# A decode step of two attention and MLP layers: kept V comes back from PSUM through ScalarE, and q is spread beside the preceding unit

## The chip, the cores and the metric

The kernel runs on one core of one Trainium2 chip. The metric is the device time of one execution in microseconds, lower is better. Where one number stands for a kernel, it is the median of its runs.

## The reference

Two layers A and B are each applied twice, with the same weights and the same caches both times. A is one decode step of attention over a cache of 4096 positions, B a small MLP block.

```python
B, D = 8, 448;  Hq, Hkv, Sk, Dh = 16, 8, 4096, 256         # bf16
def A(x, k_cache, v_cache, wq, wo):
    q = (x @ wq) as [B, 16, 1, 256]
    scores = q . k_cache[b, head // 2] * Dh ** -0.5         # two q heads share a K/V head
    p = softmax(scores)
    return (p . v_cache[b, head // 2]) as [B, 1, 4096] @ wo
def Bk(x, w1, w2, w3, w4):                                   # S == 1: the shifted branch through w1, w2 is zero
    x1 = x
    return x1 + gelu(layernorm(x1) @ w3) @ w4
x = x + A(layernorm(x));  x = x + Bk(layernorm(x))
x = x + A(layernorm(x));  x = x + Bk(layernorm(x))
```

K and V of one batch row are 16.8 MB each. Both passes need all of them, and SBUF holds about one pair of K/V heads' worth at a time beside the weights, so nearly everything is read from HBM twice.

## The kernel before

**Units, chunks, items.** A *unit* is `(ps, b, gp)`: pass 0 or 1, batch row b, and one of four pairs of K/V heads (`GP = 4`). K and V of a unit are cut into four chunks of 1 MB each, `[128, 4096]` bf16. An *item* is `(n, kv, c)`: unit number n, K (0) or V (1) or a weight block (2), and chunk c. The list `items` is the order of all work, 527 items, written out ahead of time by `block`, `weights` and `first_kept`; the main loop walks it once. Each engine executes its instructions in the order in which this loop issues them.

**Places.** 17 places in SBUF (`NC = 17`, tile `places`) hold one chunk each. `emit_loads` runs at the end of every item. It sends the next loads of the list `loads` to free places, all from SyncE's queue (L839 for a pair of K chunks in two neighbouring places, 2 MB; L870 for one chunk; L873 for halves of a chunk; L867 and L868 for the chunk called `part`). A load waits in SyncE's queue until the last reader of its place is done, and everything behind it in that queue waits too. Where two K chunks of a unit shall lie side by side (`paired`), `place_for` holds back until two neighbouring places are free.

**What is kept from pass 0 to pass 1.** Of the units with gp 2 and 3 (`keep`), pass 1 of a row follows soon after its pass 0, so their data stay: 14 chunks in places (`kept`, asked for with `stays`), chunk 1 of V of gp 2 (`inner`) whole in the PSUM banks `store[0..3]`, and 6 of the 16 position groups of chunk 0 of V of gp 3 (`part`) in `store[4]` and half of the bank `sc`, while the other 10 groups lie in the SBUF tile `rest`. `away` and `part_away` (L937, L958) copy them into PSUM with VectorE transposes of 32-bit words in pass 0, after the chunk's own PV. `back` and `part_back` (L944, L962) copy them back with the same transposes in pass 1. They are called together, after the scores of chunks 0 and 1 of unit gp 2:

```python
            if (ps, gp, c) == (1, keep[0], 1):
                where[(b, part[0]), part[1:]] = part_place
                part_back(slots[part_place])
                where[(b, inner[0]), inner[1:]] = kept_place
                back(slots[kept_place])
```

The two places for that (`kept_place`, `part_place`) are those of K chunk 0 of gp 2 and K chunk 2 of gp 3, which are not given to new loads in the meantime.

**One unit.** For a K chunk that was loaded, VectorE transposes it in place in 32x32 blocks (L902, three instructions per chunk). TensorE computes scores into the bank `sc` (L917): 32 matmuls of 256 columns where two chunks lie in neighbouring places, and twice 32 matmuls of 128 columns otherwise. After every second chunk ScalarE does exp out of `sc` (L926). Then TensorE transposes P into the bank `misc` (L969), ScalarE copies it out (L976) and prepares P of one V chunk at a time in `ptw` (L1108), one V chunk ahead, and TensorE does the PV product with 16 matmuls (L986). Before a unit's scores, `give_q` lays out its q in one of four tiles `qbd`: four small matmuls into `misc` (L370), then four VectorE casts out of it (L376). One such layout serves two units.

**A batch row's round.** The units with gp 0 and 1 of several rows are read ahead. Then come gp 2 and 3 of the row in pass 0, and a run of V chunks loaded in halves (`narrow`), during which TensorE also works through the row's generator `chain`: normalising the heads, wo, the MLP, layer norms and the next q (L174, L529 and others; its `step` is called between the items). Then gp 3 and gp 2 of the same row follow in pass 1 out of what was kept, and their V chunks are interleaved with the next unit's K. For rows 3, 5, 7 and the last, a weight block wq is loaded again and q of earlier rows is computed in between (`weights("q", ...)`, L350, L885 to L892).

Of the kernel before, what the change touches and what calls it, by code (L numbers as in the profile page):

```python
# [10 lines left out]
U32 = mybir.dt.uint32  # L11
# [6 lines left out]
def kernel(  # L18
# [621 lines left out]
    AFTER = 10  # L640

    def block(k, v=None):

        fresh = [(number[v], 1, c) for c in range(4)] if v else []
        if k is None:
            due.extend(fresh)
            items.extend(due)
            due.clear()
            return
        number[k] = len(tasks)  # L650
        tasks.append(k)
# [97 lines left out]
    def late(it):  # L749

        n, kv, c = it
        return kv == 0 and paired(n, c) and not (tasks[n][0] == 1 and stays(it))

    used_at = {it: k for k, it in enumerate(items)}
    for it in items:
# [5 lines left out]
    for b in range(Bn):  # L761
        again[(b, keep[0]), 0, 0] = again[(b, inner[0]), *inner[1:]]
        again[(b, keep[1]), 0, 2] = again[(b, part[0]), *part[1:]]
    free_at = [-1] * NC
# [168 lines left out]

    def away(slot):

        for n in range(4):
            nc.vector.transpose(  # L937
                store[n][:].bitcast(U32), slot[:].bitcast(U32)[:, 512 * n : 512 * n + 512]
            )

    def back(slot):

        for n in range(4):
            nc.vector.transpose(  # L944
                slot[:].bitcast(U32)[:, 512 * n : 512 * n + 512], store[n][:].bitcast(U32)
            )

    def part_words(slot):

        w = slot[:].bitcast(U32)  # L950
        return [
            (sc[:, 256 : 256 + 128 * (PR - 4)], w[:, 512 : 128 * PR]),
            (store[4][:], w[:, 0:512]),
        ]

    def part_away(slot):
        for kept_words, words in part_words(slot):
            nc.vector.transpose(kept_words.bitcast(U32), words)  # L958

    def part_back(slot):  # L960
        for kept_words, words in part_words(slot):
            nc.vector.transpose(words, kept_words.bitcast(U32))  # L962

# [106 lines left out]

    def give_q(who):

# [16 lines left out]
        q_of[k] = who  # L1089
        run(spread_q(who[1], who[2], qbds[k]))  # L1090

# [3 lines left out]
    v_items = [it for it in items if it[1] == 1]  # L1095
    v_next = dict(zip(v_items, v_items[1:]))
    plain = {it for it in v_items if (tasks[it[0]][:2] == (1, Bn - 1)) and tasks[it[0]][2] in free}

# [14 lines left out]
    for idx, it in enumerate(items):  # L1113
# [20 lines left out]
        if kv == 2:  # L1134
# [9 lines left out]
            elif c == 1:  # L1144
# [15 lines left out]
                )  # L1160
                project_rows(q_of_block, 0, *rows, ps_q)
        elif kv == 0:
            if (ps, b) not in state:
# [15 lines left out]
            if not kept_now:  # L1179
                transpose_k(slot)  # L1180
            if not alone:
                step(idx)
# [26 lines left out]
        else:  # L1209
            st = state[ps, b]  # L1210
            if it in narrow and it[2] == 0 and not alone and any(e["kind"] == "chain" for e in gens):
                alone.append(n)
# [26 lines left out]
            else:  # L1239
# [5 lines left out]
                alone_now = (ps, b) in split and gp in free  # L1245
                if c == 0:
                    o_of[n] = st["o", g8]
                o_now = o_of[n]
                if c == 0 and (alone_now or pairs_done.get((ps, b), 0) % 2 == 1):
                    done = pairs_done[ps, b] + 1  # L1250
# [20 lines left out]
                if ps == 0 and inside(it):  # L1271
                    away(slot)
                if ps == 0 and halfway(it):
                    part_away(slot)
            if c == 3:
                pairs_done[ps, b] = pairs_done.get((ps, b), 0) + 1
                free_slots.append(slot_of.pop(n))
# [176 lines left out]
```

## Time and profile before

| | |
|---|---|
| median of 3 runs | 1065.47 us (1064.1 to 1067.35) |
| profiled execution | 1061.72 us, its span 1059.6 us |
| busy: TensorE, VectorE, ScalarE | 627.0, 616.4, 161.7 us of the span |
| mean granted TensorE clock | 0.678 |
| read from HBM | 424.22 MB, 400 GB/s over the span |

The profile is one execution on the chip. Its times are in us, those of single instructions in ns. In a group's row stand the line, the engine, the operation, what it writes and reads, the count, the busy time and the mean of one, and then the engine's idle time just before such instructions with what ended it. PE is TensorE, PEld its weight loads, DVE VectorE, ACT ScalarE, POOL GpSimd, SP SyncE, and SPq what SyncE's queue does. The chain is the work that ended last, followed back from the end.

### The profile page before, as it was taken

The numbers are of one execution on the slowest core, as the hardware profiler recorded it, in microseconds if no ns is written. First come the engines' busy times: TensorE is split into PE (matmuls) and PEld (weight loads), VectorE is DVE, ScalarE is ACT, GpSimd is POOL, SyncE is SP. The second block draws the span as 40 slices with busy tenths as digits, with TensorE's granted clock in tenths as the row PEclk, the third lists the DMA queues.
The fourth block names the chain that finished last, engine by engine and source line by source line (L and its number), as shares of the span: only waits on it lengthen the run. The fifth ranks groups of instructions, "written<-read, shape, count | busy, mean of one in ns | idle before, by whom it ended". The sixth has DMA issues, their size and how long they took to land.

```text
span 1059.6 us, 29163 instructions
## 1 busy us (share of the span) xinstructions
PE 627.0 (59%) x12932; PEld 395.0 (37%) x12932; DVE 616.4 (58%) x1319; ACT 161.7 (15%) x613; POOL 16.4 (2%) x27
## 2 busy tenths in 40 slices
PE   3144457655575547664586566656764666657675
PEld 2022225432343324442343234423442444434455
DVE  5146862578527882467628952785288437792362
ACT  1011110211111111111112111111111111111110
POOL 0000000000000000000000000000000000000000
PEclk9999996665675656657656566656665686556665
DMA  9999999999999999999999999999999999999994
GB/s 300 387 424 424 424 415 388 422 421 423 401 406 426 424 420 404 409 403 424 414 389 426 425 410 410 378 425 412 401 424 423 393 389 420 423 418 348 393 416 203
DMA packets 71757, 426.11 MB, mean 402 GB/s; under 512 B 7496, under 2 KB 13520, under 8 KB 43856
## 3 DMA queue, kind: packets, MB, share of 16 engines
q1 hardware_dynamic: 71440, 424.01, 98.8%
q8 instruction: 101, 1.65, 0.6%
q10 hardware_dynamic: 192, 0.25, 0.1%
q14 instruction: 24, 0.20, 0.0%
HBM read 424.22 MB, written 0.01 MB: 400 GB/s over the span
## 4 chain that ended last, share of the span: by engine, by line
DMA 47%; DVE 24%; PE 21%; ACT 3%; issue 2%; SPq 2%; POOL 1%; DVEq 0%; ACTq 0%
DMA places<-in_A_v_cache_dram 25%; DMA places<-in_A_k_cache_dram 20%; DVE places L902 18%; PE sc L917 9%; PE o L986 7%; ACT p_n L926 2%; PE misc L174 2%; DMA places<-in_A_wq_dram 2%; PE misc L529 1%; DVE store L937 1%; DVE places L944 1%; DVE qbd L376 1%; SPq L193 1%; SPq L870 1%; ACT o_sb L523 1%
## 5 line engine op out<-in xcount | busy, mean ns | idle before, releaser
L902 DVE STREAM_TRANSPOSE places<-places 128x512 uint32<-128x512 uint32 (+1 forms) x576 | 455.5, 854 | 83.0 <-DMA places<-in_A_k_cache_dram 81.0
L917 PE MATMUL sc<-places,qbd 128*8 128x256 bf16 (+1 forms) x5024 | 246.9, 347 | 244.9 <-DVE places L902 236.1
L986 PE MATMUL o<-places,ptw 128*8 128x256 bf16 x3808 | 232.3, 369 | 101.4 <-DMA places<-in_A_v_cache_dram 70.9
L917 PEld LDWEIGHTS <-qbd 128*8 128x8 bf16 x5024 | 130.4, 104 | 327.8 <-DVE places L902 140.1
L986 PEld LDWEIGHTS <-ptw 128*8 128x8 bf16 x3968 | 103.7, 102 | 171.4 <-issue 95.8
L926 ACT ACTIVATE p_n<-sc 128x256 bf16<-128x256 f32 x128 | 95.4, 745 | 395.1 <-PE sc L917 392.4
L1108 ACT COPY ptw<-psv 128x32 bf16<-128x32 bf16 x248 | 52.6, 226 | 173.7 <-PE o L986 161.4
L976 ACT CAST psv<-misc 128x128 bf16<-128x128 f32 x64 | 17.0, 266 | 253.3 <-PE misc L969 253.3
L493 DVE RECIPROCAL rz<-misc 128x8 f32<-128x8 f32 (+1 forms) x35 | 6.7, 191 | 77.4 <-PE misc L490 77.4
L376 DVE CAST qbd<-misc 32x32 bf16<-32x32 f32 x128 | 23.2, 182 | 27.6 <-PE misc L370 26.3
L529 PE MATMUL misc<-R_t,o_sb 128*128 128x8 f32 (+1 forms) x132 | 26.7, 311 | 20.7 <-DVE R_t L515 13.9
L529 PEld LDWEIGHTS misc<-R_t,o_sb 128*128 128x128 f32 x132 | 23.8, 252 | 30.9 <-issue 17.2
L926 ACT ACTIVATION_READ_ACCUMULATOR p_n<-sc 128x1 f32 x128 | 33.8, 264 | 0.0
L174 PEld LDWEIGHTS <-w_sb 128*128 128x128 bf16 x896 | 27.3, 103 | 14.2 <-issue 13.8
L525 DVE MEMSET o<- 128x256 f32 x33 | 9.0, 272 | 35.0 <-PE o L986 31.2
L490 PE MATMUL misc<-zm,one 128*128 128x8 f32 (+1 forms) x70 | 17.1, 317 | 18.9 <-DVE zm L482 17.1
L275 POOL TENSOR_TENSOR t<-t,nhalf 128x2 f32<-128x2 f32 (+2 forms) x18 | 12.0, 670 | 957.7 <-DVE t L296 957.7
L490 PEld LDWEIGHTS misc<-zm,one 128*128 128x128 f32 x70 | 14.1, 251 | 29.1 <-issue 24.9
L969 PEld LDWEIGHTS <-p_n 128*128 128x128 bf16 x256 | 11.9, 105 | 31.6 <-issue 20.0
L969 PE MATMUL misc<-identb,p_n 128*128 128x32 bf16 x256 | 18.0, 190 | 9.3 <-ACT p_n L926 6.8
L937 DVE STREAM_TRANSPOSE store<-places 128x512 uint32<-128x512 uint32 x32 | 19.8, 686 | 0.0
L944 DVE STREAM_TRANSPOSE places<-store 128x512 uint32<-128x512 uint32 x32 | 19.7, 672 | 0.0
(150 smaller groups left out, 350.8 us busy)
## 6 DMA issues: line engine op xcount, KB each, us to landing
places<-in_A_k_cache_dram SPq DMA_DIRECT2D x62, 2048.0 KB, 17.5
places<-in_A_v_cache_dram SPq DMA_DIRECT2D x194, 512.0 KB, 7.2
places<-in_A_v_cache_dram SPq DMA_DIRECT2D x87, 1024.0 KB, 20.7
places<-in_A_k_cache_dram SPq DMA_DIRECT2D x68, 1024.0 KB, 13.3
places<-in_A_wq_dram SPq DMA_DIRECT2D x5, 1024.0 KB
rest<-in_A_v_cache_dram SPq DMA_DIRECT2D x8, 640.0 KB, 19.6
places<-in_A_wo_dram SPq DMA_DIRECT2D x5, 896.0 KB, 19.7
places<-in_A_v_cache_dram SPq DMA_DIRECT2D x8, 384.0 KB, 18.9
```

What stands on the lines that cost most here:

```text
L174: nc.tensor.matmul(bass.AP(out.tensor, out.offset, [out.ap[0], (1, WIDE)]), w, x.to_broadcast([128, WIDE]), start=start, stop=stop, skip_g ...
L376: nc.vector.tensor_copy(qbd[32 * a : 32 * a + 32, :, :, a, :], qs.rearrange("p e (f g u h) -> p (e f) u g h", f=2, u=2, h=2)[:, :, u],)
L490: nc.tensor.matmul(z_ps, ones, zm[:], start=True, stop=True)
L529: nc.tensor.matmul(ot_ps[:, j], o_sb[:].rearrange("p (i j) -> p j i", j=2)[:, j], R, start=True, stop=True)
L902: nc.vector.transpose(w, w)
L917: nc.tensor.matmul(sc[32 * k : 32 * k + 8, 128 * (x % 2) : 128 * (x % 2 + nx)], qbd[:, ep, gp % 2].rearrange("p a h -> p (a h)"), v, start ...
L926: nc.scalar.activation(p_sb[:, :, :, 2 * u : 2 * u + 2].rearrange("p t i x -> p x t i"), sc[:, 0:256].rearrange("p (x t i) -> p x t i", x= ...
L937: nc.vector.transpose(store[n][:].bitcast(U32), slot[:].bitcast(U32)[:, 512 * n : 512 * n + 512])
L944: nc.vector.transpose(slot[:].bitcast(U32)[:, 512 * n : 512 * n + 512], store[n][:].bitcast(U32))
L969: nc.tensor.matmul(pt_ps[:, t], p_sb[:, t].rearrange("p i x -> p (i x)"), cols, start=True, stop=True,)
L986: nc.tensor.matmul(o_ps[32 * q : 32 * q + 8, :], ptz[:, at : at + 8], v[:, y * Dh : (y + 1) * Dh] if v2 is None or y < PR else v2[:, (y - ...
L1108: nc.scalar.copy(ptw[:, ring_of[it], :, 6:8], psv[slot_of[it[0]]][:, it[2]])
```

## The change

Five things change. The line numbers above are those of the kernel before.

1. In pass 1 the V chunks of gp 2 and gp 3 are taken in another order (`v_order`): `inner` and `part` come last in their units.
2. Into PSUM they now go by a VectorE OR with 0 on 32-bit words, out of PSUM by ScalarE copies of bf16, one per bank: four pieces of 1024 elements for `inner`, one of 1024 and one of 512 for `part`. The list `moves` holds the pieces, and the main loop issues one at the end of each item.
3. The places that they return to are those of V chunks 1 and 2 of gp 3 (`homes`), after their PV. K chunk 0 of gp 2 and K chunk 2 of gp 3 are free for loads as soon as their scores are done.
4. `q_ahead` starts the layout of the next unit's q at chunk 2 of the preceding unit (the four matmuls), and chunk 3 of that unit does the four casts after its own transposes. It leaves out units whose q is not there yet.
5. What began or ended a unit's V at chunk 0 or 3 now does so at the first or last V chunk in the new order.

```diff
+    def v_order(v):
+        for chunk in (inner, part):
+            if v[0] == 1 and v[2] == chunk[0]:
+                return [c for c in range(4) if c != chunk[2]] + [chunk[2]]
+        return range(4)
     def block(k, v=None):
-        fresh = [(number[v], 1, c) for c in range(4)] if v else []
+        fresh = [(number[v], 1, c) for c in v_order(v)] if v else []
...
+    homes = v_order((1, 0, keep[1]))[:2]
-        again[(b, keep[0]), 0, 0] = again[(b, inner[0]), *inner[1:]]
-        again[(b, keep[1]), 0, 2] = again[(b, part[0]), *part[1:]]
+        again[(b, keep[1]), 1, homes[0]] = again[(b, part[0]), *part[1:]]
+        again[(b, keep[1]), 1, homes[1]] = again[(b, inner[0]), *inner[1:]]
...
-    def away(slot):
-        for n in range(4):
-            nc.vector.transpose(
-                store[n][:].bitcast(U32), slot[:].bitcast(U32)[:, 512 * n : 512 * n + 512]
-            )
+    def inner_words(slot):
+        return [(store[n][:], slot[:, 1024 * n : 1024 * n + 1024]) for n in range(4)]
     def part_words(slot):
         return [
+            (store[4][:], slot[:, 0:1024]),
+            (sc[:, 256 : 256 + 128 * (PR - 4)], slot[:, 1024 : PR * Dh]),
         ]
+    def away(pieces):
+        for kept_words, words in pieces:
+            nc.vector.tensor_single_scalar(
+                kept_words.bitcast(U32), words.bitcast(U32), 0, op=ALU.bitwise_or
+            )
+    def back(kept_words, words):
+        nc.scalar.copy(words, kept_words.bitcast(BF16))
+    def move(all_of=False):
+        while moves:
+            back(*moves.pop(0))
+            if not all_of:
+                break
...
+    def q_ahead(idx):
+        seen = []
+        for m, kv, c in items[idx + 1 :]:
+            ps, b, gp = tasks[m]
+            if kv or m in seen or m == items[idx][0]:
+                continue
+            seen.append(m)
+            who = (ps, b, gp // 2)
+            if who in q_of:
+                if len(seen) == 2:
+                    return
+                continue
+            if ps == 1 and (gp in keep or b not in q_rows_done):
+                return
+            q_begun.append(give_q(who, True))
+            return
...
             if not kept_now:
                 transpose_k(slot)
+            if c == 3 and q_begun:
+                run(q_begun.pop())
...
+            if c == 2:
+                q_ahead(idx)
...
-            if (ps, gp, c) == (1, keep[0], 1):
-                where[(b, part[0]), part[1:]] = part_place
-                part_back(slots[part_place])
-                where[(b, inner[0]), inner[1:]] = kept_place
-                back(slots[kept_place])
         else:
             st = state[ps, b]
+            if ps == 1 and (halfway(it) or inside(it)):
+                while moves and any(w.offset == v.offset for _, w in moves for _, v in (part_words if halfway(it) else inner_words)(slot)):
+                    move()
...
-            if (ps, gp, kv, c) == (1, keep[0], 0, 0):
-                kept_place = p
-            elif (ps, gp, kv, c) == (1, keep[1], 0, 2):
-                part_place = p
+            if (ps, gp, kv, c) == (1, keep[1], 1, homes[0]):
+                where[(b, part[0]), part[1:]] = p
+                moves.extend(part_words(slot))
+            elif (ps, gp, kv, c) == (1, keep[1], 1, homes[1]):
+                where[(b, inner[0]), inner[1:]] = p
+                moves.extend(inner_words(slot))
...
         emit_loads()
+        move()
         step(idx, it in narrow)
```

More of the change, by code (lines that the diff above doesn't have):

```diff
@@ L752, in late @@
         return kv == 0 and paired(n, c) and not (tasks[n][0] == 1 and stays(it))
+    homes = v_order((1, 0, keep[1]))[:2]
+    assert part[0] == keep[1] and inner[0] == keep[0]
     used_at = {it: k for k, it in enumerate(items)}
@@ L932, in exps, with part_words @@
         )
-    def away(slot):
-        for n in range(4):
-            nc.vector.transpose(
-                store[n][:].bitcast(U32), slot[:].bitcast(U32)[:, 512 * n : 512 * n + 512]
-            )
[L941 to L945, printed above, removed]
-            )
[L948 to L962, printed above, removed]
+    def inner_words(slot):
+        return [(store[n][:], slot[:, 1024 * n : 1024 * n + 1024]) for n in range(4)]
+    def part_words(slot):
+        return [
+            (store[4][:], slot[:, 0:1024]),
+            (sc[:, 256 : 256 + 128 * (PR - 4)], slot[:, 1024 : PR * Dh]),
+        ]
+    def away(pieces):
+        for kept_words, words in pieces:
+            nc.vector.tensor_single_scalar(
+                kept_words.bitcast(U32), words.bitcast(U32), 0, op=ALU.bitwise_or
+            )
+    def back(kept_words, words):
+        nc.scalar.copy(words, kept_words.bitcast(BF16))
+    moves = []
+    def move(all_of=False):
[3 more added lines that the diff above has]
+                break
     def transpose_p(p_sb, p_to):
@@ L1069, in step, with give_q @@
                     gens.remove(e)
-    def give_q(who):
+    q_rows_done = set()
+    q_begun = []
+    def q_ahead(idx):
[14 more added lines that the diff above has]
+            return
+    def give_q(who, begin=False):
         first = next((i[0] for i in items[now[0] :] if i[1] == 0), 0)
@@ L1089, in give_q @@
         q_of[k] = who
-        run(spread_q(who[1], who[2], qbds[k]))
+        g = spread_q(who[1], who[2], qbds[k])
+        if begin:
+            next(g)
+            return g
+        run(g)
     o_of = {}
@@ L1096 @@
     v_next = dict(zip(v_items, v_items[1:]))
+    v_last = {it[0]: it for it in v_items}
+    v_first = {it[0]: it for it in v_items[::-1]}
     plain = {it for it in v_items if (tasks[it[0]][:2] == (1, Bn - 1)) and tasks[it[0]][2] in free}
@@ L1161 @@
                 project_rows(q_of_block, 0, *rows, ps_q)
+                if idx > 1:
+                    q_rows_done.update(range(*rows))
         elif kv == 0:
@@ L1245 @@
                 alone_now = (ps, b) in split and gp in free
-                if c == 0:
+                if it == v_first[n]:
                     o_of[n] = st["o", g8]
                 o_now = o_of[n]
-                if c == 0 and (alone_now or pairs_done.get((ps, b), 0) % 2 == 1):
+                if it == v_first[n] and (alone_now or pairs_done.get((ps, b), 0) % 2 == 1):
                     done = pairs_done[ps, b] + 1
@@ L1271 @@
                 if ps == 0 and inside(it):
-                    away(slot)
+                    away(inner_words(slot))
                 if ps == 0 and halfway(it):
-                    part_away(slot)
-            if c == 3:
+                    away(part_words(slot))
+            if it == v_last[n]:
                 pairs_done[ps, b] = pairs_done.get((ps, b), 0) + 1
```

## The prediction

> **What bounds the kernel now.** I read the page's first lines, its slices and queue table, then its chain.
>
> ```profile
> span 1059.6 us, 29163 instructions
> PE 627.0 (59%) x12932; PEld 395.0 (37%) x12932; DVE 616.4 (58%) x1319; ACT 161.7 (15%) x613; POOL 16.4 (2%) x27
> GB/s 300 387 424 424 424 415 388 422 421 423 401 406 426 424 420 404 409 403 424 414 389 426 425 410 410 378 425 412 401 424 423 393 389 420 423 418 348 393 416 203
> q1 hardware_dynamic: 71440, 424.01, 98.8%
> DMA 47%; DVE 24%; PE 21%; ACT 3%; issue 2%; SPq 2%; POOL 1%; DVEq 0%; ACTq 0%
> ```
>
> The queue that brings K and V fills the 16 DMA engines for 98.8% of the span, and its best slices move 424 to 426 GB/s. At that rate 424 MB alone take 1000 us. No engine's own 58 or 59% is the limit. Work saved on VectorE or TensorE shortens the span only where it closes a dip of this stream. So I looked for the dips with a table by stage (columns: stretch, its length, the engines' busy time and counts, granted clock, DMA share, GB/s).
>
> ```profile
> 160.00:170.00 10.00, 8.37 (x192) 5.76 (x195) 2.79 (x16) 0.98 (x5) 0.71 (x1) 0.90 0.98 358
> 530.00:550.00 20.00, 15.86 (x326) 9.62 (x322) 4.34 (x24) 1.64 (x8) 0.61 (x2) 0.50 1.00 384
> 665.00:671.00 6.00, 2.15 (x40) 1.29 (x37) 3.72 (x8) 1.08 (x5) 0.00 (x0) 0.50 1.03 317
> 671.00:677.00 6.00, 4.83 (x92) 2.56 (x92) 6.00 (x9) 1.27 (x5) 0.00 (x0) 0.54 0.92 348
> 677.00:700.00 23.00, 15.15 (x323) 9.19 (x315) 19.97 (x37) 4.38 (x17) 0.00 (x0) 0.64 1.00 421
> 930.00:953.00 23.00, 13.42 (x284) 8.15 (x287) 22.38 (x35) 3.66 (x12) 0.00 (x0) 0.50 1.01 417
> 953.00:968.00 15.00, 11.00 (x236) 7.30 (x229) 4.02 (x19) 3.16 (x13) 0.70 (x1) 0.73 0.86 304
> 968.00:985.00 17.00, 13.28 (x290) 8.33 (x293) 3.68 (x21) 1.42 (x7) 0.55 (x1) 0.50 1.02 405
> 1047.00:1059.00 12.00, 5.97 (x176) 5.04 (x176) 4.15 (x24) 0.50 (x2) 1.99 (x2) 0.50 0.02 5
> ```
>
> Only two dips inside have DMA engines truly idle (share 0.92 and 0.86). Dip B, 671 to 677, lost (421 - 348) / 421 x 6 = 1.0 us. Dip A, 953 to 968, against the 405 that the same half loads reach right after it, lost (405 - 304) / 405 x 15 = 3.7 us. At 665 to 671 the engines were full (1.03) while small wq transfers went through: that stays. After 1047 no data move and some 12 us of closing arithmetic follow, which the change does not touch. The chain shows what made dip A (start, length, what).
>
> ```profile
> 869.39 1.05 DVE places L962 x2
> 870.44 2.39 DVE places L944 x4
> 906.96 8.19 DVE places L902 x10
> 946.88 4.71 DVE places L902 x6
> 955.26 1.03 PE o L986 x16
> 961.32 6.80 DMA places<-in_A_v_cache_dram
> ```
>
> From 869 to 961 the chain holds no transfer: computing had fallen behind, so V places came free late and the stream ran dry. The copying back of kept V (L962, L944) is in that chain. In earlier rows a chain piece of DMA follows before the run of V, so computing waits for data there and its savings are swallowed.
>
> **The change part by part.**
>
> ```profile
> L902 DVE STREAM_TRANSPOSE places<-places 128x512 uint32<-128x512 uint32 (+1 forms) x576 | 455.5, 854 | 83.0 <-DMA places<-in_A_k_cache_dram 81.0
> L937 DVE STREAM_TRANSPOSE store<-places 128x512 uint32<-128x512 uint32 x32 | 19.8, 686 | 0.0
> L944 DVE STREAM_TRANSPOSE places<-store 128x512 uint32<-128x512 uint32 x32 | 19.7, 672 | 0.0
> L962 DVE STREAM_TRANSPOSE places<-sc 128x256 uint32<-128x256 uint32 x8 | 3.6, 450 | 14.1 <-ACT ptw L1108 7.6 <-ACT p_n L926 6.5
> L130 DVE MEMSET sc<- 128x512 f32 x1 | 0.5, 485 | 0.1
> L1108 ACT COPY ptw<-psv 128x32 bf16<-128x32 bf16 x248 | 52.6, 226 | 173.7 <-PE o L986 161.4 <-PE misc L370 10.9
> L523 ACT COPY o_sb<-o 128x256 f32<-128x256 f32 x33 | 12.7, 384 | 17.8 <-PE o L986 17.6
> DVE qbd L376 <- PE misc L370: 26.3, 31, 3.6
> ```
>
> *Back, off VectorE.* Per batch row 1.05 + 2.39 = 3.44 us leave VectorE's queue, 27.5 us over eight rows.
>
> *Away.* Six transposes become six OR with 0 of the same words. The trace has no such operation. Nearest is the transpose it replaces, 686 ns (same places, same shape), then the memset into the same kind of bank, 485 ns; the dearest row of such a word count is the transpose of K, 854 ns. I take no change, by the row with the same operands; the ends, for five and a half such pieces, are -1.1 us and +0.9 us per row.
>
> *Back, on ScalarE.* From 32 elements in 226 ns and 256 in 384 ns come 0.705 ns an element: 1024 bf16 cost 0.93 us, 512 cost 0.56 us. Five large and one small piece are 5.2 us per row, 42 us in all, on an engine busy for 161.7. One piece goes out after each item; behind it in ScalarE's queue stand the next exp (L926) and the next copy of P (L1108), for which TensorE's scores and PV wait. I take it as hidden, because ScalarE is idle 85% of the span; uncovered, it is the third rival's price.
> The Trainium skill (ScalarE: Activation LUTs, What ACT_TABLE_LOAD costs) speaks against this part: ScalarE does one element per cycle whatever the type, 186 ns + 0.833 ns each, so two bf16 per word double its count. By it, as an estimate, a large piece costs 1.04 us and a row 5.8 us; the rows above bear out the per-element cost, a little lower.
>
> *q beside the preceding unit.* The changed program begins 21 of the 32 spreads early; 8 stay in the chain of the row and 3 find no predecessor or no q yet. The four casts stay; what goes is VectorE's wait for the four matmuls, 26.3 / 31 = 0.85 us each. Two begun ones lie in dip A's lead-up: 1.7 us. TensorE's next use of the misc bank now waits until VectorE has passed a K tile and the casts. In the lead-up TensorE waits for VectorE anyway.
>
> *Places.* In each row the places of two kept K, held until now for the V that comes back, are free at once; V chunks 1 and 2 of the first kept unit hold theirs instead, from a later item on. In the changed program's listing most K loads behind that point go out one to seven items sooner; in two rows some go three items later. Eight score groups lose their neighbour: 16 matmuls 128 wide take 0.60 and 256 wide 1.02, so a split group of 32 adds about 0.4 us, 2.9 us in all, spread over the rows.
>
> ```profile
> 945.14 0.60 PE L917 MATMUL sc<-places,qbd 128*8 128x128 bf16 x16 [0.87 <-ACT p_n L926]
> 923.06 1.02 PE L917 MATMUL sc<-places,qbd 128*8 128x256 bf16 x16
> 657.64 7.90 SPq L870 DMA_DIRECT2D places<-in_A_k_cache_dram  x2
> 673.87 2.24 SPq L839 DMA_DIRECT2D places<-in_A_k_cache_dram  x2
> ```
>
> *Dip B.* SP issued a K tile that ended at 665.5 and nothing more until 673.87; the queue ran low. The next K pair, issued at item 322 before, goes out at items 316 and 317 in the changed program, as single tiles into kept K's places, ahead of the gap. I count the whole 1.0 us as gained.
>
> *Dip A.* VectorE's lead-up loses 3.44 + 1.7 = 5.1 us, but its last two K tiles (L902 x6, 946.88) cannot be taken before they land.
>
> ```profile
> 904.89 0.33 SPq L839 DMA_DIRECT2D places<-in_A_k_cache_dram  x1
> places<-in_A_k_cache_dram SPq DMA_DIRECT2D x1, 2048.0 KB, 29.5
> 909.79 14.67 SPq L870 DMA_DIRECT2D places<-in_A_k_cache_dram  x2
> 933.77 0.33 SPq L839 DMA_DIRECT2D places<-in_A_k_cache_dram  x1
> ```
>
> The pair issued at 904.89 landed 29.5 us later, at 934.4. Behind it in the queue are two tiles of 1024 KB and the last pair, 4.19 MB; at the 417 GB/s of that stretch they take 10.1 us and land at 944.5. So VectorE gains 946.88 - 944.5 = 2.4 us, not 5.1. V places come free 2.4 us sooner and dip A shrinks from 3.7 to 1.3 us.
>
> **Sum.** 1.0 + 2.4 = 3.4 us. The profiled execution took 1061.72 us (span 1059.6 and 2.1 around it), so 1058.3. The median of the runs is 1065.47, 3.75 above it; I carry the difference over: 1062.1 us.
>
> **The rivals.**
> 1. *The stream hides nearly everything.* If dip A is set by the rhythm of freed V places (SP waits, PV, next half) and not by the entry, only B closes: -1.0 us, 1064.5. For it: the runs of V at 160 and 530 dip too, at full DMA share. Against: the share of 0.86 is found at A alone.
> 2. *Runs of V gain as well.* If earlier loads and a freer VectorE lift the four runs like the first and last shown (160 to 170, 280 to 300, 420 to 430, 530 to 550; 358 to 384 GB/s) to 405, that is 1.2 + 1.0 + 0.5 + 1.0 = 3.7 us more: 1058.4. Against: TensorE, not VectorE, is busy there.
> 3. *ScalarE's in-order queue becomes the wait (slower).* A piece moved back must wait for the PV that empties its new place, 1.03 us at L986, and then runs 0.93. If all six stand between scores and exp in a lead-up, that is 6 x 1.96 = 11.8 us against 5.1 removed: dip A grows by 6.7 us and B gains nothing, 1072.2. It decides from the point where the exposed part of the 11.8 exceeds 5.1. For it: exp already sits in the chain. Against: moves go one to an item, and exps only at every second K.
> 4. *It does not do what it says.* The order gets worse, not better: the loads sent three items later in two rows open a dip of one tile each, 1.05 MB at 421 GB/s or 2.5 us: 5.0 - 3.4, 1067.1. Against: the same rows have loads sent earlier just ahead.
>
> **How the numbers follow.** Forecast 0.45, rivals 0.13, 0.15, 0.19 and 0.08. The forecast's own range, from away's ends and from dip A closing by half or wholly, is 1059.7 to 1063.5. 0.3%, 3.2 us, is about what a measurement of this kernel can tell from no change; the forecast lies just past it, so I put 0.31 of its 0.45 above and 0.14 below. Faster: with rival 2, 0.46. Same: with rivals 1 and 4 (+1.6 us), 0.35. Slower: rival 3, 0.19. The range reaches from rival 2 with away's gain (1058.4 - 1.1, 1057.3) past rival 4 with away's loss (1067.1 + 0.9, 1068.0); what it leaves out is rival 3 beyond 2.5 us.
>
> **What would show it.** L944 and L962 gone from VectorE; 48 copies on ScalarE at 0.56 and 0.93 us; L376's wait near 10 us; 348 at dip B risen to some 420 and 304 at dip A to some 365 GB/s; slices elsewhere as before; the closing 12 us unchanged. It is wrong if a new dip below 380 GB/s appears between rows, if exp (L926) waits in the chain behind a copy, or if the time falls by more than 7 us, which no dip seen here can give.

## The result, and the profile after

The changed kernel takes 1061.58 us (median of 20 runs, 1060.45 to 1065.16) against 1065.72 us of the kernel before in 20 runs beside it: ratio 0.9965, 95% interval 0.9956 to 0.9975. That is 3.7 us less, or 4.1 by the medians. The same kernel beside other runs of before gave 0.9975 (0.9962 to 0.9987; e12 below). The forecast was 1062.1 us.

The two profiled executions can't be compared by their spans: that of before (1061.72 us) is one of its quickest, that of after (1063.68 us, span 1061.6) one of its slower ones. Stages are compared instead. First the page of after: span, busy times, GB/s in 40 slices, the queue that brings K and V, and the chain's shares.

```profile
span 1061.6 us, 29691 instructions
PE 624.7 (59%) x13188; PEld 395.1 (37%) x13188; DVE 588.4 (55%) x1271; ACT 201.8 (19%) x661; POOL 16.4 (2%) x27
GB/s 300 390 425 423 424 416 373 422 424 423 394 411 426 424 419 389 415 398 423 410 372 423 424 412 397 396 421 408 384 425 423 409 385 417 423 419 383 392 416 198
q1 hardware_dynamic: 72448, 424.01, 98.8%
DMA 57%; DVE 18%; PE 17%; issue 2%; SPq 2%; ACT 2%; POOL 1%; DVEq 0%; POOLq 0%; ACTq 0%
```

The stream is as before: 424.01 MB at 98.8%. VectorE lost 28 us, ScalarE gained 40. In the chain DMA rose from 47 to 57%, and VectorE and TensorE fell by 6 and 4 points: the kernel waits more for data and less for itself. The slice that holds most of dip A (the 37th) went from 348 to 383 GB/s. The same in the table by stage (stretch, length, busy times and counts of PE, PEld, DVE, ACT, POOL, granted clock, DMA share, GB/s), after:

```profile
671.00:677.00 6.00, 4.16 (x132) 3.07 (x135) 5.89 (x10) 3.65 (x7) 0.00 (x0) 0.75 1.04 350
738.00:765.00 27.00, 20.64 (x477) 13.73 (x480) 6.05 (x34) 2.42 (x12) 1.26 (x2) 0.69 0.99 377
930.00:953.00 23.00, 12.66 (x288) 7.81 (x287) 21.93 (x34) 3.65 (x12) 0.00 (x0) 0.50 1.01 419
953.00:968.00 15.00, 11.17 (x220) 7.12 (x221) 4.64 (x19) 3.15 (x13) 0.62 (x1) 0.73 0.97 382
1049.00:1061.00 12.00, 5.97 (x176) 5.04 (x176) 4.15 (x24) 0.50 (x2) 2.00 (x2) 0.50 0.02 5
```

and one stage of before that the prediction did not show, the run of V halves that follows dip B:

```profile
738.00:765.00 27.00, 19.73 (x418) 12.77 (x421) 5.96 (x34) 3.59 (x15) 1.25 (x2) 0.68 1.02 399
```

Dip A went from a DMA share of 0.86 to 0.97. Dip B's share is 1.04: the engines no longer stand still there (the 350 GB/s come with 122 of wq's packets of 2 KB, which now fall into this stretch; in before 128 of them fell into 665 to 671). But the run of V behind it fell from 399 to 377 GB/s. The busy times of the closing 12 us are the same to a hundredth. Rows of the chain into dip A, after (in the changed kernel L911 is the transposes of K, L926 the scores, L935 exp, L994 PV, L957 the copying away and L962 the copying back):

```profile
928.96 2.44 DVE store L957 x4
931.45 18.08 DMA places<-in_A_k_cache_dram
949.56 3.57 DVE places L911 x4
953.17 1.91 PE sc L926 x29
956.79 1.03 PE o L994 x13
962.78 7.42 DMA places<-in_A_v_cache_dram
```

In before, the chain from 869 to 961 held no transfer. Now a K load of 18.08 us stands in it, and VectorE takes the last K tiles 0.03 us after they land. The copies, from the groups by line of after:

```profile
L962 ACT COPY places<-store 128x1024 bf16<-128x1024 bf16 x40 | 40.2, 1031 | 17.2 <-PE o L994 17.2
L962 ACT COPY places<-sc 128x512 bf16<-128x512 bf16 x8 | 4.9, 617 | 0.0
L957 DVE TENSOR_SCALAR store<-places 128x512 uint32<-128x512 uint32 x40 | 24.9, 679 | 0.2
L957 DVE TENSOR_SCALAR sc<-places 128x256 uint32<-128x256 uint32 x8 | 3.4, 428 | 7.9 <-ACT p_n L935 7.9
```

and q's casts, from its waits (us in total, times, longest):

```profile
DVE qbd L376 <- PE misc L370: 34.1, 17, 9.1
```

### The profile page after: what moved, and what is told of

Its sections match the earlier page's. It is cut to its first block, busy times and chain, and to the rows that moved or that the text cites. A ratio compares the mean times of both kernels' runs of the same rounds, so it can differ in the third digit from the quotient of the medians.

```text
span 1061.6 us, 29691 instructions
## 1 busy us (share of the span) xinstructions
PE 624.7 (59%) x13188; PEld 395.1 (37%) x13188; DVE 588.4 (55%) x1271; ACT 201.8 (19%) x661; POOL 16.4 (2%) x27
## 3 DMA queue, kind: packets, MB, share of 16 engines
q1 hardware_dynamic: 72448, 424.01, 98.8%
## 4 chain that ended last, share of the span: by engine, by line
DMA 57%; DVE 18%; PE 17%; issue 2%; SPq 2%; ACT 2%; POOL 1%; DVEq 0%; POOLq 0%; ACTq 0%
DMA places<-in_A_k_cache_dram 34%; DMA places<-in_A_v_cache_dram 22%; DVE places L911 15%; PE o L994 6%; PE sc L926 5%; PE misc L174 3%; PE misc L529 1%; ACT p_n L935 1%; SPq L879 1%; DVE store L957 1%; SPq L193 1%; DMA places<-in_A_wq_dram 1%; PE misc L490 1%; DVE qbd L376 1%; POOL t L275 0%
## 5 line engine op out<-in xcount | busy, mean ns | idle before, releaser
L911 DVE STREAM_TRANSPOSE places<-places 128x512 uint32<-128x512 uint32 (+1 forms) x576 | 457.0, 855 | 121.4 <-DMA places<-in_A_k_cache_dram 119.1
L926 PE MATMUL sc<-places,qbd 128*8 128x128 bf16 (+1 forms) x5280 | 246.5, 336 | 227.5 <-DVE places L911 215.1
L994 PE MATMUL o<-places,ptw 128*8 128x256 bf16 x3808 | 231.8, 368 | 133.2 <-DMA places<-in_A_v_cache_dram 95.8
L926 PEld LDWEIGHTS <-qbd 128*8 128x8 bf16 x5280 | 134.2, 103 | 306.5 <-DVE places L911 127.3
L994 PEld LDWEIGHTS <-ptw 128*8 128x8 bf16 x3968 | 101.8, 101 | 202.4 <-issue 123.6
L935 ACT ACTIVATE p_n<-sc 128x256 bf16<-128x256 f32 x128 | 95.2, 744 | 356.9 <-PE sc L926 355.7
L962 ACT COPY places<-store 128x1024 bf16<-128x1024 bf16 x40 | 40.2, 1031 | 17.2 <-PE o L994 17.2
L376 DVE CAST qbd<-misc 32x32 bf16<-32x32 f32 x128 | 22.7, 178 | 35.4 <-PE misc L370 34.1
L935 ACT ACTIVATION_READ_ACCUMULATOR p_n<-sc 128x1 f32 x128 | 33.8, 264 | 0.0
L957 DVE TENSOR_SCALAR store<-places 128x512 uint32<-128x512 uint32 x40 | 24.9, 679 | 0.2
```

What stands on the lines that cost most here:

```text
L376: nc.vector.tensor_copy(qbd[32 * a : 32 * a + 32, :, :, a, :], qs.rearrange("p e (f g u h) -> p (e f) u g h", f=2, u=2, h=2)[:, :, u],)
L911: nc.vector.transpose(w, w)
L926: nc.tensor.matmul(sc[32 * k : 32 * k + 8, 128 * (x % 2) : 128 * (x % 2 + nx)], qbd[:, ep, gp % 2].rearrange("p a h -> p (a h)"), v, start ...
L935: nc.scalar.activation(p_sb[:, :, :, 2 * u : 2 * u + 2].rearrange("p t i x -> p x t i"), sc[:, 0:256].rearrange("p (x t i) -> p x t i", x= ...
L957: nc.vector.tensor_single_scalar(kept_words.bitcast(U32), words.bitcast(U32), 0, op=ALU.bitwise_or)
L962: nc.scalar.copy(words, kept_words.bitcast(BF16))
```

## The experiments

Three parts of the change can carry the gain: VectorE's relief, the other places, the early q. And three things can take it back: ScalarE's queue, the new order, the stream itself.

One table serves all. The stages are times between equal byte counts of the stream: the moments at which the packets of q1 begun so far reach a given sum, so a stage always holds the same bytes; its ends are named by their times in before. Before is shown in us, the others as the difference from it. *Lag*: loads go through one queue in the order of issue, so the byte count at which each is complete is known; the lag is its landing less the moment at which the stream reaches that count, here for the loads that land around 730 us. The last two columns are windows of the profile. Each row is one profiled execution; the ratio is over all runs.

| kernel | ratio (95%) | 655–700 (dip B) | 727–765 (run of V) | 945–985 (dip A) | lag, us | GB/s 738–765 | GB/s 953–968 |
|---|---|---|---|---|---|---|---|
| before | | 45.00 | 37.94 | 40.01 | 1.7 | 399 | 304 |
| e5 before again | 1.0006 (0.9992–1.0021) | +1.26 | −0.12 | −0.84 | 1.7 | 401 | 354 |
| e2 early q only | 1.0003 (0.9987–1.0019) | −1.04 | +0.18 | +0.70 | 1.8 | 401 | 303 |
| e7 before, back by ScalarE | 1.0022 (1.0006–1.0037) | +1.54 | −0.25 | +1.50 | 1.8 | 407 | 314 |
| e4 no back but in row 6 | 1.0001 (0.9986–1.0015) | −0.94 | +2.74 | −0.43 | 2.8 | 360 | 363 |
| e6 after, back by VectorE | 1.0004 (0.9989–1.0019) | −1.67 | −0.23 | −1.88 | 2.0 | 403 | 353 |
| e9 after, old places | 0.9984 (0.9972–0.9997) | −1.72 | −0.40 | −0.53 | 1.6 | 407 | 316 |
| e3 no back in row 6 | 0.9973 (0.9958–0.9989) | +0.03 | +0.17 | −2.24 | 2.1 | 396 | 388 |
| after | 0.9965 (0.9956–0.9975) | −0.87 | +1.55 | −2.38 | 2.7 | 377 | 382 |
| e12 after again | 0.9975 (0.9962–0.9987) | −1.11 | +0.55 | −2.86 | 2.6 | 390 | 385 |
| e1 after, no early q | 0.9967 (0.9954–0.998) | −1.55 | +1.44 | −2.38 | 3.1 | 379 | 379 |
| e8 after, copies twice | 0.9985 (0.9974–0.9996) | −1.30 | +1.35 | −3.54 | 2.7 | 379 | 406 |
| e10 away split | 0.9975 (0.9961–0.9989) | −1.22 | +0.49 | −2.62 | 2.4 | 390 | 385 |
| e11 as words | 0.9986 (0.9972–1.0) | −1.18 | +1.08 | −2.93 | 2.4 | 385 | 403 |

**e1, the changed kernel without the early q.**

```diff
-            if c == 2:
-                q_ahead(idx)
```

> The change without the early q: copies back on ScalarE, new V order, new places. Theory (the two dips of the transfer stream): dip B closes by the earlier loads (-1.0 us) and dip A's lead-up on VectorE gets 3.44 us shorter, more than the 2.4 us that landing data allow, so the whole -3.4 us is there: ratio to before 0.997, as for the full change. Rival (q's early spread carries it): about half or less of the gain, 0.9985 or above. Rival (ScalarE's queue is a wait of its own, masked by the early q): at or above 1.000.

0.9967, the same as the changed kernel. Dip A closes alike (−2.38 us in both). The early q carries none of the gain that the intervals let one see.

**e2, the kernel before with the early q alone** (`q_ahead`, and `give_q` in two steps).

> The kernel before with the early q alone; V comes back on VectorE as before. Theory: dip A's lead-up loses two waits of 0.85 us and nothing else, dip B stays: -1.7 us at most, ratio 0.9984 to 1.000, dip A's stretch up from 304 GB/s to about 350. Rival (q carries the gain): 0.9965. Rival (casts behind a K tile hold the misc bank): above 1.001.

1.0003, and dip A at 303 GB/s. The waits of the casts in e2:

```profile
DVE qbd L376 <- PE misc L370: 31.3, 16, 9.0
```

Before it was 26.3 us in 31 waits of 3.6 at most. The early q halves the number of waits, but their sum rises: a begun spread that VectorE reaches ahead of its matmuls holds it for up to 9 us.

**e3, before with the copying back left out in row 6** (the V that it would bring back in that row is not there).

```diff
+                if b != 6:
                     part_back(slots[part_place])
...
+                if b != 6:
                     back(slots[kept_place])
```

> The kernel before, with the copying back of kept V left out for batch row 6 alone (its V is then not the right data); nothing else. That is the copy in dip A's lead-up, 3.44 us of VectorE. Theory: 2.4 us gained (landing data stop the rest), ratio 0.9977, dip A's stretch from 304 GB/s to about 365, dip B unchanged near 348. Rival 1 (dip A follows the rhythm of the freed places): 0.9995 to 1.000 and dip A unchanged.

0.9973 from one row in eight, 2.9 us (1.2 to 4.5). Its chain into dip A ends in a landing, as in after, and VectorE starts 0.03 us behind it:

```profile
933.88 14.59 DMA places<-in_A_k_cache_dram
948.50 1.00 DVE places L902
```

**e4, before with the copying back left out in all rows but row 6** (seven rows lack that V).

```diff
+                if b == 6:
                     part_back(slots[part_place])
...
+                if b == 6:
                     back(slots[kept_place])
```

> The kernel before, with the copying back left out for every batch row but 6 (their V is then not the right data), seven times 3.44 us of VectorE. Theory: computing waits for data in these rows, so only dip B gains, through the earlier end of the K transposes before it: -1.0 us, ratio 0.999, dip A unchanged near 304 GB/s. Rival (saved VectorE time counts wherever it is): -24 us at most, ratio 0.98 to 0.995, or at least seven eighths of the gain of the full change.

1.0001: some 23 us taken off VectorE (616.4 to 593.7) in seven rows are worth nothing that the interval (1.5 us less to 1.6 us more) lets one see. Dip B closes all the same, and the run of V behind it is 2.74 us longer. Windows of e4:

```profile
671.00:677.00 6.00, 5.27 (x115) 3.11 (x116) 4.72 (x8) 2.15 (x9) 0.00 (x0) 0.77 1.04 345
738.00:765.00 27.00, 19.70 (x436) 13.49 (x437) 6.06 (x34) 2.73 (x13) 1.25 (x2) 0.69 0.99 360
```

So e3 and e4 put the gain at dip A, as far as intervals of 1.5 us tell.

**e5, the kernel before once more.** The same program, for a second profile.

> The kernel before once more, for a second profile of one and the same program. Both theories: ratio 1.000 within 0.002. If the dip at 953 to 968 us is a property of the program, it shows again at 290 to 320 GB/s with a DMA share near 0.86, and the times between equal byte marks of the stream from 945 to 985 differ by under 0.4 us from the first profile. If the single runs of V and dip B wander from execution to execution, stages such as 655 to 700 and 727 to 765 differ by 0.5 to 1.5 us between the two profiles; if they do not wander (under 0.3 us), then what the changed kernel lost at 727 to 765 (+1.55 us) was its own doing.

1.0006, but the stages wander: dip B by 1.26 us, dip A by 0.84. The window of dip A in e5 moves 354 GB/s where the first profile had 304:

```profile
953.00:968.00 15.00, 10.85 (x228) 7.12 (x229) 6.20 (x20) 3.16 (x13) 0.00 (x0) 0.72 0.93 354
```

A single stage of a single profile is therefore good to about 1 us. What did not wander is the kind of chain: in e5 too it holds no transfer, there from 864 to 963 us.

**e6, the changed kernel, pieces back by VectorE.**

```diff
-        nc.scalar.copy(words, kept_words.bitcast(BF16))
+        nc.vector.tensor_single_scalar(
+            words.bitcast(U32), kept_words.bitcast(U32), 0, op=ALU.bitwise_or
+        )
```

> The changed kernel, but its pieces come back by VectorE (OR with 0) in place of ScalarE; order, places and early q stay changed. If the lightened VectorE ahead of the row at 869 to 961 us carries the gain: 3.4 us per row return to VectorE, 1.7 of the 5.1 us stay saved, dip A closes by at most 1.7 us, ratio 0.9985 to 1.000. If the other places and the other order carry it: the ratio stays at 0.9965, with 380 GB/s at 953 to 968. If VectorE's copies cost more than the transposes did, as they now stand one after each item between K tiles: over 1.000.

1.0004: with VectorE doing the copies, new places, new order and early q together gain nothing over the whole execution. Dip A is partly closed all the same: its stage is 1.88 us shorter than in the first profile of before. But from the stream's last bytes to the end e6 takes some 1.7 us longer than before, with VectorE's copies in the chain of the last row. The lead-up's chain is VectorE again, 18 transposes in one go with no landing in it. The window of dip A, then two rows of the chain:

```profile
953.00:968.00 15.00, 11.84 (x268) 8.18 (x269) 3.64 (x20) 3.03 (x13) 0.70 (x1) 0.82 0.95 353
```

```profile
936.94 13.96 DVE places L911 x18
950.94 1.91 PE sc L926 x32
```

**e7, the kernel before, pieces back by ScalarE** at the point where the transposes stood, all six in one go. The copying away becomes the OR with 0 of the changed kernel. Of the edit, the four large pieces back:

```diff
-            nc.vector.transpose(
-                slot[:].bitcast(U32)[:, 512 * n : 512 * n + 512], store[n][:].bitcast(U32)
-            )
+            nc.scalar.copy(slot[:, 1024 * n : 1024 * n + 1024], store[n][:].bitcast(BF16))
```

> The kernel before, with one thing changed: away is an OR with 0 and back is six ScalarE copies (five of 1.03 us and one of about 0.6 us, 5.8 us in one go per row) at the place in the order where the transposes stood. Places, order and q stay as before. If VectorE's relief alone carries the gain: VectorE gets 3.44 us sooner to the K tiles of the next row, dip A closes by 2 to 2.4 us, ratio 0.9970 to 0.9980. If the new places and order carry it: 1.000. If ScalarE's in-order queue is the danger (rival 3 of the prediction): the next exp stands behind 5.8 us of copies, more than the 3.44 us removed, dip A grows by 1 to 2.4 us, ratio 1.001 to 1.002.

1.0022 (1.0006 to 1.0037): a little slower, the sign of the prediction's rival 3. The chain of e7 shows it: the exp, then 5.0 us of copies in place of 3.44 of transposes, then ScalarE's next work, with TensorE waiting for it.

```profile
870.29 0.26 ACT p_n L926
870.55 1.33 ACT places L963 x2
871.88 3.67 ACT places L945 x4
875.55 0.29 ACT o_sb L523
875.88 1.02 PE misc L529 x4
```

**e8, the changed kernel with each copy issued twice.**

```diff
-        nc.scalar.copy(words, kept_words.bitcast(BF16))
+        for _ in range(2):
+            nc.scalar.copy(words, kept_words.bitcast(BF16))
```

> The changed kernel with each ScalarE copy issued twice: 48 more copies, some 46 us more on ScalarE, 5.8 us in each row, in front of the same exps and copies of P. If the copies are hidden, as the prediction has it: ratio 0.9965 within 0.001, dip A as in the changed kernel (380 GB/s). If ScalarE's in-order queue already takes part of the gain (rival 3): each doubled piece adds up to 1 us in the lead-up, 3 to 5.8 us at dip A, ratio 0.999 to 1.002.

0.9985, between the two expectations: 44 us more on ScalarE (201.8 to 245.5) cost about 1.1 us against e12's ratio and 2.1 against the first; the intervals overlap. Dip A stays closed (406 GB/s), though copies stand in the chain of its row too, 5.7 us of them between 883 and 889: a K load of 17.75 us follows at 928 and ends that part of the chain. The loss that this profile shows lies in the last row, where the chain holds no load behind the copies. Rows of the chain of e8 there:

```profile
1024.35 0.92 ACT places L963
1025.29 1.01 ACT places L963
1026.31 0.64 ACT p_n L935 x2
1026.95 0.86 ACT places L963
1027.83 1.01 ACT places L963
1029.02 1.02 PE o L995 x11
```

Copies stand before the exp and before the copy of P for which the PV product waits, and the stretch from the stream's last bytes to the end is some 1.7 us longer than before's, as in e6. In the changed kernel the chain at that place is a transfer, and that stretch is within 0.2 us of before's.

**e9, the changed kernel with the old places.** The pieces go to the K places that before used, as soon as those are scored; all else stays changed.

```diff
...
+            if (ps, gp, c) == (1, keep[0], 1):
+                where[(b, part[0]), part[1:]] = part_place
+                where[(b, inner[0]), inner[1:]] = kept_place
+                moves.extend(part_words(slots[part_place]))
+                moves.extend(inner_words(slots[kept_place]))
...
-            if (ps, gp, kv, c) == (1, keep[1], 1, homes[0]):
-                where[(b, part[0]), part[1:]] = p
-                moves.extend(part_words(slot))
-            elif (ps, gp, kv, c) == (1, keep[1], 1, homes[1]):
-                where[(b, inner[0]), inner[1:]] = p
-                moves.extend(inner_words(slot))
+            if (ps, gp, kv, c) == (1, keep[0], 0, 0):
+                kept_place = p
+            elif (ps, gp, kv, c) == (1, keep[1], 0, 2):
+                part_place = p
```

> The changed kernel with one part undone: the pieces return to the two K places that the kernel before used, held until then, and no longer to the places of two V chunks. ScalarE, one piece after each item, V's order and the early q stay changed. If VectorE's relief with copies spread over the items carries the gain: dip A (953 to 968 us) stays near 380 GB/s and the stage 945 to 985 about 2.4 us shorter than before, while dip B (671 to 677) opens again to a DMA share of 0.92; ratio 0.9965 to 0.998. If the early free K places carry it: ratio 0.999 to 1.001 and dip A near the 304 to 354 GB/s of the two profiles of before.

0.9984, and the opposite of what was expected in detail: dip B closes and dip A does not.

```profile
671.00:677.00 6.00, 4.48 (x136) 2.76 (x138) 5.97 (x11) 1.77 (x6) 0.00 (x0) 0.83 1.03 397
953.00:968.00 15.00, 12.01 (x259) 8.01 (x260) 3.40 (x18) 2.85 (x13) 0.70 (x1) 0.73 0.92 316
```

The chain of e9 says why dip A stays open. The old places are ready early, so the pieces are issued between the scores and their exps:

```profile
869.07 0.85 ACT places L962
872.63 0.58 ACT places L962
873.22 0.64 ACT p_n L935 x2
873.86 0.85 ACT places L962
874.87 1.02 PE o L994 x16
```

2.28 us of copies stand in the chain where 3.44 us of transposes stood, and from there to 967 it holds no K load. In the changed kernel no copy is in that stretch of the chain: the new places come free only after the PV of two V chunks, when these exps are over. That e9 is slower than e12 (0.9984 against 0.9975) is inside both intervals; the chains differ clearly, the times do not. And 0.9984 (0.9972 to 0.9997) is a gain of 0.3 to 3.0 us with dip A open, for which the account by dip A alone has no place.

**e10, every second piece of the copying away by ScalarE. e11, as e10, and the pieces come back as 512 words instead of 1024 bf16.** The last two lines are e11's alone.

```diff
+        for n, (kept_words, words) in enumerate(pieces):
+            if n % 2:
+                nc.scalar.copy(kept_words.bitcast(FP32), words.bitcast(FP32))
+                continue
...
-        nc.scalar.copy(words, kept_words.bitcast(BF16))
+        nc.scalar.copy(words.bitcast(FP32), kept_words.bitcast(FP32))
```

> The changed kernel with every second piece of the copying away done by ScalarE, so two of inner's four and the small one of part. In the changed kernel's chain a K load of 18.08 us follows VectorE's four pieces (L957, 2.44 us at 928.96). Half of them on ScalarE at 0.55 us each (0.186 + 512 elements) give the place back about 1.1 us sooner and take 1.6 us per row off VectorE. If the lead-up is bound by that load's landing and landing by the bytes queued ahead of it, as the prediction has it: no change, ratio 0.9965 within 0.001. If the load's issue decides: up to 1.1 us more at dip A, ratio 0.9955.

> As the one before, and ScalarE also brings the pieces back as 32-bit words: half as many elements, 0.55 us in place of 1.03 for a large piece, about 22 us less on ScalarE. If ScalarE's copies are hidden in the changed kernel: no change against that, 0.9965 within 0.001. If some of their price still shows, as doubling them cost 0.0020 of the time: the reverse of it, half as large, ratio 0.995 to 0.9955. If loads are held by ScalarE's share of the copying away: 0.998 or more.

0.9975 and 0.9986 beside 0.9975 of the changed kernel in the same set: neither helps. Both take 1.0 us longer from the stream's last bytes to the end (12.9 us against 11.9), so the ratio alone does not tell what they do at dip A. The stage does: −2.62 and −2.93 us, beside −2.38 and −2.86 of the changed kernel. In e10 VectorE is 12 us lighter, and the chain into dip A is the same K load:

```profile
929.96 18.44 DMA places<-in_A_k_cache_dram
```

It is bound by its landing; more relief buys nothing at dip A, as the prediction's step there had it. Expected were 0.55 us for 512 words by ScalarE; they took 0.59 us into PSUM and 0.60 out of it. No version tried is faster than the changed kernel beyond the intervals.

**e12, the changed kernel once more.**

> The changed kernel once more, for a second profile and as the one against which the three others of this set are read. Ratio 0.9955 to 0.9975. If loads land later than their bytes because single DMA engines are held by instruction packets (16 KB in 1.07 to 1.10 us), the run of V at 738 to 765 goes with that lag and not with the program: near 400 GB/s if the loads of 724 to 737 land 2.1 us or less after their bytes, near 380 if 2.7 us or more. If the give-back there (1.55 us) is the program's own: again about 380 GB/s whatever the lag.

0.9975. Windows of the second profile, then a row of its chain:

```profile
738.00:765.00 27.00, 20.71 (x495) 14.08 (x498) 5.79 (x33) 2.86 (x13) 1.25 (x2) 0.69 1.01 390
953.00:968.00 15.00, 11.05 (x226) 6.81 (x215) 4.11 (x20) 3.15 (x13) 0.70 (x1) 0.73 1.00 385
```

```profile
930.33 18.02 DMA places<-in_A_k_cache_dram
```

Dip A is closed again and the same load stands in the chain. The run of V lies at 390 GB/s with a lag of 2.6 us, between the 360 to 379 at 2.7 to 3.1 and the 396 to 407 at 2.1 or less. That fits the expectation by the lag better than the one by the program (about 380 whatever the lag), but 2.6 lies between the two cases that it named.

## Why the prediction was right, point by point

**Sign and place of the main term: right; size within what one profile tells.** Dip A was to shrink by 2.4 us; it did by 2.38 and 2.86 against the first profile of before, by 1.5 and 2.0 against its second. e3 shows that the copying back in that one row is the cause (2.9 us, 1.2 to 4.5), and e4 that the other seven rows are worth no more than 1.5 us. The kernels of all seven profiles with a K load in the chain between 928 and 950 (after, e1, e3, e8, e10, e11, e12) stand at 0.9965 to 0.9986; of the seven without one, before aside, five stand at 1.000 to 1.002 and e9 at 0.9984. The limit was also right: the last K pair is taken 0.03 us after landing, and 12 us more relief (e10) moved the stage no further. That the first pair of profiles gives the forecast 2.4 us almost to the hundredth is luck, since the four pairs range from 1.5 to 2.9.

**What the term needs: seen too narrowly.** The prediction took the VectorE time removed as enough. e7 and e9 show that it is not: moved to ScalarE at the old point or to the old places, the copies stand before the exps, and dip A stays open. e6 shows that the new places without ScalarE do only part of it: 353 GB/s, no K load in the chain, and no gain in the ratio. Of the versions that bring all of V back, only those with both have the K load in the chain. The rival with ScalarE's in-order queue was real. What keeps it off, by the chains of e9 and of the changed kernel, is that the new places come free late; the prediction did not make this argument (it counted on one move per item).

**Dip B: closed as forecast, but the 1.0 us is not shown.** The size was read too high: a share of 0.92 over 6 us leaves 0.08 x 6 = 0.5 us of idle engines, and the 1.0 us came from the rate. Nor do the runs show the gain. In the first profile of after, dip B and the run of V behind it together are 0.68 us longer than in the first of before, in the second 0.56 us shorter; against the second profile of before both are shorter, by 0.46 and 1.70. Of the four kernels that close dip B without the K load at dip A, e2, e4 and e6 stand at 1.0003, 1.0001 and 1.0004 with intervals of about 1.6 us to either side, and e9 at 0.9984. So what dip B is worth stays open. K loads into kept K's places, the reason named for its closing, are not needed for it either: e9 closes it without them, e2 with the early q, e4 by leaving VectorE's copies out.

That the run of V is longer by 0.49 to 2.74 us in after, e1, e4, e8, e10, e11 and e12 goes with the lag. Over the 14 profiles the rate at 738 to 765 is 396 to 407 GB/s at a lag of 2.1 us or less and 360 to 390 at 2.4 or more. The closing of dip B does not explain the lag: for the first load that lands behind it, between 683 and 688 us, the lag is 1.5 to 2.0 us in e1, e8, e10, e11 and e12, 2.4 in after and 2.6 in e4, against 2.1 to 2.4 in the four profiles in which dip B is open. It rises behind that, and the last section says what goes by there. e2, e6 and e9 close dip B and keep 1.6 to 2.0 around 730 us.

**Away: right.** 679 ns in place of 686, no change.

**Back on ScalarE: mis-sized, without effect.** I took 0.93 and 0.56 us from two rows; it is 1.031 and 0.617 us, 45.1 us in all instead of 42. The Trainium skill (ScalarE: Activation LUTs, What ACT_TABLE_LOAD costs) gives 186 ns and 0.833 ns an element for an ACTIVATE with immediate scale and bias, as an estimate 1.04 and 0.61 us for these copies: the trace agrees within 1%. "Hidden" holds at dip A, where the chain of after has no copy; elsewhere that chain has one, 0.85 us at 780.18. Doubled, they stand in the chain of dip A's row too (e8).

**Early q: wrong.** I counted 1.7 us in the lead-up, which the landing swallowed in the sum anyway, and said that L376's wait would fall to 10 us. It rose from 26.3 to 34.1. Alone it is worth nothing (e2), and without it the change is worth the same (e1).

**The rest.** The closing 12 us are unchanged, as forecast. Rival 2 (runs of V gain too) did not come: by equal bytes the six stretches of before at 157 to 187, 278 to 310, 400 to 432, 520 to 552, 620 to 655 and 727 to 765 us take up to 1.5 us more and nowhere 0.1 us less in the two profiles of after than in the first of before. One sign of being wrong, a new dip below 380 GB/s between rows, was met by the 377 at 738 to 765 of the first profile of after and not by the 390 of the second; the kernel was faster all the same. The split score groups (2.9 us of TensorE by the estimate) and the new order of V were not tried by themselves; TensorE's busy time did not rise (627.0, then 624.7 us). Without dip B's 1.0 us the steps give 2.4 us; measured are 2.7 and 3.7, and intervals of 1 us on either side do not say whether that 1.0 us, or something else of its size, is missing.

## What to carry to other kernels

Where one transfer stream is the bound, work taken off an engine paid here only in the row in which the chain held no transfer, and only until the next load landed: find that row first, and test it by leaving the work out there alone. A copy that moves to an idle engine with an in-order queue pays or costs by what it stands in front of; let its target come free late enough that the urgent instructions are already through. A stage of one profile that gains or loses 1 us is no evidence until the same program has been profiled twice.

## What the runs showed of the hardware

One program's stages differ from execution to execution by a larger share than its total does: between the two profiles of before dip B's stage differs by 1.26 of 45 us, 2.8%, and the whole execution by 4.3 of 1062 us, 0.4%. The same dip A moved 304 and 354 GB/s, while the ratio of the two sets was 1.0006. One thing that takes part in it is in the queue table of before:

```profile
q8 instruction: 101, 1.65, 0.6%
```

101 packets of 16 KB bring instructions, and 0.6% of 16 engines over 1059.6 us is 1.0 us for each; single ones in the trace of before take 0.88 to 1.32 us. A load lands when the last engine has brought its share: the Trainium skill (DMA: Bandwidth & Descriptors, Why a DMA increments its semaphore by 16 and not by 1) says that up to 16 engines finish independently and the semaphore counts them. The trace agrees: of the 16 increments that each load makes, the last comes 1.3 to 4.5 us after the first in before, and the lags of 1.1 to 3.8 us there rise with it (correlation 0.88 over 216 loads). For the loads around 730 us this spread is 1.9 us in before, 3.8 in after and 3.9 in e1.

The increments also show a single engine falling behind. In before, the last two increments of the load that lands at 731.9 us come 0.02 us apart. An instruction packet of 1.03 us starts at 736.98, and at the next load, 739.4, the last increment comes 1.02 us after the fifteenth; the lag rises from 1.7 to 2.7. In after such a packet at 715.6 us is followed by a rise of the lag from 2.2 to 2.9 us between the loads that land at 716 and 719; in e1 two at 713.3 and 722.4 by one from 1.7 to 3.1. Not every packet does it: behind one at 724.6 in before and one at 719.6 in e9 the lag does not rise. That these packets cause the rises was not tried.
